# The float64 weights of a recurrence-attention-MLP kernel: converted in the recurrence's last unit but one, and kept in DRAM as float32

## The chip, the cores and the metric

The kernel runs on one core of a Trainium2 chip. The core has five engines, each with a queue of its own that it works through in order: TensorE (PE, matrix products; its weight loads are listed as PEld), VectorE (DVE), ScalarE (ACT), GpSimd (POOL) and SyncE (SP), which here only issues transfers (DMAs). Engines wait for each other through semaphores. The metric is the time of one execution on the device in microseconds (us).

## What is computed

Three parts, one behind the other, in float32:

```python
# r, k, v, w, a, b: (4, 8, 768, 40)
for t in range(S):                                   # recurrence, per batch and head
    y[:, :, t] = rt @ state
    Sa = state @ at
    state = state * wt - outer(Sa, bt) + outer(vt, kt)
x = y as (4, 768, 320)
# mixture of attention experts: x @ w_gate picks 2 of 4 experts; each is causal attention
out += weight_e * (softmax(causal(q_e k_e^T / 8)) @ v_e) @ wo[e]
# gated MLP with mixing over the sequence
h = relu(out @ w_in);  u, v = h[..., :512], h[..., 512:]
v_s = w_spatial @ layernorm(v) + b_spatial
result = (u * v_s) @ w_out
```

`w_in` (320 x 1024) and `w_out` (512 x 320) arrive as float64; all else is float32.

## The kernel before

**The recurrence** (`recurrence`) cuts the sequence into chunks of 64 positions. Two batches with eight heads go together; three chunks make a unit, and there are 8 units (counted from 0), so 24 steps. For each unit a preparation `p1` builds what the steps need, one unit ahead and more: among it `p_l` and `p_sub`, the solve of triangular 32 x 32 systems for all heads at once: 31 pairs of DVE instructions, `sub = L * X` (L227) and `X = X - sub` (L229), each pair on the result of the last. All their operands lie in SBUF. A step `p2` carries the state: PE makes a product, ACT copies it back (`wsb`, L374, L391, L400; `VU`, L393, L407), PE uses it for the next, and at its end DVE adds and scales the new state `SV` (L419, L420), with which the next step's products begin (L370). Beside the state, the outputs of the step before are made: `am` on DVE is a product under a mask (L322), PE needs it in L333 and L341, and `xs` (L344) is stored to `xd` in DRAM.

**Order.** PE's order is written out by hand (`manual_schedule`): after each part of a step `pump` is called, five times a step, 15 times a unit; it runs what of `p1` is due, and other work. The orders of DVE, ACT, POOL and SP are decided when the program is built, by a scheduler that estimates times. On the chip each engine then works through its row in order, and an instruction that waits holds up all behind it.

**Beside the last two units.** In unit 6, whose three steps are the last with a solve in them (that of unit 7), `pump` also advances `pre()`: it loads and splits the weights `wq`, `wk`, `wv`, `w_gate` (`attn_prep`: twelve loads of L629 and L630, then casts and subtractions on DVE, `wv_h`, `wq_l` and so on) and the first batch of x (`first_x`: `xf`, `xh`, `xl`). In unit 7 the attention of batch 0 runs between the steps (`tail`), and `wout_prep` makes `wu_h` and `wu_l` of `w_out`, in four pieces of 128 x 320.

**Behind the recurrence** the rest of that attention is blended with `mlp_prep`, which loads `b_spatial` and `wo`, multiplies `wo` with `w_in` on PE (L701) into `wc_h` and `wc_l` (twelve pieces of `w_in`, 256 columns each), and turns `w_spatial` (L713). Then MLP and attention of the four batches are blended until the end.

**The conversion** of one piece of float64 is `load_f64`: a load of the raw words on SP (L572), three ACT instructions (L578, L579, L581: low word scaled, sign, magnitude), four on DVE (L582 to L585, the bit work) and three on POOL (L586 to L588, products and sum in float32). POOL's take two operands from SBUF and write SBUF.

```python
hi = raw.bitcast(F32).rearrange("p (n w) -> p n w", w=2)[:p, :, 1]
nc.scalar.mul(m, lo, 2.0 ** -52)
nc.vector.tensor_scalar(ei, ti, 1, 0x7F800000, op0=OP.logical_shift_right, op1=OP.bitwise_and)
nc.gpsimd.tensor_mul(m, m, e)
```

## Time and profile before

| | us |
|---|---|
| median of 3 runs | 1215.08 |
| lowest, highest | 1214.11, 1222.42 |
| the profiled execution | 1223.75 |
| its span, first to last instruction | 1222.0 |

Busy time of the span: PE 1024.8 us (84%), DVE 761.9 (62%), ACT 652.1 (53%), POOL 203.0 (17%). Unit 6 lies at about 562 to 627 us, unit 7 at 627 to 735, the attention's tail behind it to about 747, the preparation of the MLP to about 816, then the blended main part.

A row of the timeline gives an instruction's start and duration in us, the engine, the line, what it writes and reads, how many instructions are merged in the row, and in brackets the time the engine had stood before it and what ended that. PEclk is the TensorE clock that was granted, as a share of its full 2.4 GHz; 0.50 is its lower level of 1.2 GHz.

### The profile page before, as it was taken

The page shows a single profiled execution, that of the slowest core. Times are in us where ns is not written, and L with a number is a line of the kernel's source. Part 1 is how long each engine was busy: PE and PEld are TensorE (multiplying, and loading weights), DVE is VectorE, ACT ScalarE, POOL GpSimd, SP SyncE. Part 2 cuts the span into 40 slices and gives each one's busy share as a digit, 9 for nine tenths or more (in the row PEclk, how much of TensorE's full clock was granted, in tenths as well). Part 3 has the DMA queues.
Part 4 walks back from the last instruction along what each step waited for, and adds up shares of the span by engine and source line. Part 5 has one row for each costly group of instructions (what it writes and reads, how often), then busy time and mean ns, then how long its engine had stood idle before and what let it go on. Part 6 is the DMA issues. An engine that isn't in the chain of part 4 may idle for free.

```text
span 1222.0 us, 31926 instructions
## 1 busy us (share of the span) xinstructions
PE 1024.8 (84%) x12730; PEld 896.5 (73%) x12730; DVE 761.9 (62%) x1930; ACT 652.1 (53%) x1599; POOL 203.0 (17%) x381
## 2 busy tenths in 40 slices
PE   5757787787887969879797877798999899999998
PEld 3546676777776868768685665576898798789888
DVE  4586739467495474854835446988657656765650
ACT  2345564655645557465455445667555556555641
POOL 5011000010010100000002015802211211121131
PEclk9999767666766566676675766799999999989999
DMA  4333343333333333323211103210000001000000
GB/s 64 61 63 62 53 67 62 54 57 55 69 60 57 56 52 69 64 45 80 53 41 33 28 7 107 68 39 1 18 32 17 1 17 49 1 1 17 18 1 33
DMA packets 214663, 52.96 MB, mean 43 GB/s; under 512 B 204785, under 2 KB 210673, under 8 KB 214514
## 3 DMA queue, kind: packets, MB, share of 16 engines
q1 hardware_dynamic: 214514, 50.92, 21.2%
q8 instruction: 100, 1.64, 0.6%
q14 instruction: 49, 0.40, 0.1%
HBM read 39.07 MB, written 7.86 MB: 38 GB/s over the span
## 4 chain that ended last, share of the span: by engine, by line
PE 48%; DVE 28%; ACT 14%; issue 5%; DMA 3%; POOL 2%; SPq 1%; ACTq 0%; DVEq 0%; POOLq 0%
DVE X L229 5%; DVE sub L227 5%; PE mm L952 4%; PE mm L953 4%; PE mm L954 4%; ACT XTD L196 3%; ACT XTD L241 3%; PE p L141 2%; PE mp L911 2%; PE y L333 2%; PE mp L841 2%; PE pw L404 2%; PE y L341 2%; ACT f L881 2%; PE p L217 2%
## 5 line engine op out<-in xcount | busy, mean ns | idle before, releaser
L141 PE MATMUL p<-ident,slab 96*128 96x96 f32 x512 | 102.4, 340 | 43.7 <-ACT XTD L197 20.0
L141 PEld LDWEIGHTS p<-ident,slab 96*128 96x128 f32 x512 | 73.7, 194 | 60.7 <-ACT XTD L197 22.4
L227 DVE TENSOR_TENSOR sub<-L,X 96x31 f32<-96x31 f32 (+15 forms) x248 | 83.4, 336 | 17.0 <-ACT L L218 10.5
L196 ACT COPY XTD<-p 32x192 f32<-32x192 f32 x64 | 30.6, 479 | 110.4 <-DVE WL L193 109.9
L229 DVE TENSOR_TENSOR X<-X,sub 96x31 f32<-96x31 f32 (+15 forms) x248 | 83.1, 335 | 6.0
L881 ACT ACTIVATE f<-sc,nm 128x512 f32<-128x512 f32 (+2 forms) x110 | 59.4, 544 | 31.6 <-DVE nm L876 14.4
L602 DVE TENSOR_TENSOR ptl<-mp,pth 128x256 fp32r<-128x256 f32 (+2 forms) x126 | 57.0, 460 | 23.1 <-ACT pth L601 22.1
L876 DVE TENSOR_REDUCE nm<-sc 128x1 f32<-128x512 f32 (+2 forms) x110 | 54.6, 505 | 22.9 <-PE sc L874 18.6
L333 PE MATMUL y<-RT,S 40*40 40x64 f32 (+1 forms) x768 | 49.5, 308 | 22.4 <-DVE am L322 22.4
L159 DVE TENSOR_TENSOR_SCAN PP<-W,scan 104x390 f32<-104x390 f32 x32 | 30.9, 966 | 58.4 <-ACT W L157 58.4
L601 ACT CAST pth<-mp 128x256 fp32r<-128x256 f32 (+2 forms) x126 | 50.0, 409 | 32.3 <-PE mp L911 18.4
L202 POOL COPY PEN<-PP 40x6 f32<-40x6 f32 x64 | 25.7, 401 | 245.0 <-DVE PP L159 243.6
L333 PEld LDWEIGHTS y<-RT,S 40*40 40x40 f32 (+1 forms) x768 | 43.2, 194 | 25.6 <-DVE am L322 23.7
L193 DVE TENSOR_TENSOR WL<-p,mask 64x384 f32<-64x384 f32 x32 | 17.9, 560 | 67.6 <-PE xt L189 67.1
L316 PE MATMUL y<-RT,vut 40*64 40x64 f32 x1536 | 48.1, 259 | 12.2 <-ACT S L383 11.8
L911 PE MATMUL mp<-ident,f 128*128 128x128 f32 x294 | 51.5, 295 | 4.6 <-DVE f L897 2.3
L920 PE MATMUL pa<-pth,vv 128*128 128x256 f32 x168 | 47.5, 297 | 5.9 <-DVE at L932 3.8
L316 PEld LDWEIGHTS y<-RT,vut 40*64 40x64 f32 x1536 | 37.7, 164 | 19.0 <-ACT S L383 14.7
L952 PE MATMUL mm<-ws_h,vn_h 128*128 128x384 f32 x144 | 49.2, 341 | 0.4 <-ACT vn_h L601 0.3
L171 DVE TENSOR_TENSOR kb<-p,RPE 104x384 f32<-104x384 f32 x64 | 35.2, 554 | 22.4 <-PE p L141 20.9
L897 DVE TENSOR_SCALAR f<-f,sm 128x128 f32<-128x128 f32 (+2 forms) x96 | 45.3, 513 | 5.9 <-POOL sm L889 5.3
L953 PE MATMUL mm<-ws_l,vn_h 128*128 128x384 f32 x144 | 48.6, 338 | 0.0
(284 smaller groups left out, 3122.1 us busy)
## 6 DMA issues: line engine op xcount, KB each, us to landing
slab<-in_w_dram SPq DMA_DIRECT2D x128, 30.0 KB
slab<-in_b_dram SPq DMA_DIRECT2D x128, 30.0 KB
slab<-in_k_dram SPq DMA_DIRECT2D x128, 30.0 KB
slab<-in_a_dram SPq DMA_DIRECT2D x128, 30.0 KB
SV<-in_v_dram SPq DMA_DIRECT2D x48, 80.0 KB
VU<-in_v_dram SPq DMA_DIRECT2D x48, 80.0 KB
RR<-in_r_dram SPq DMA_DIRECT2D x48, 80.0 KB
WL<-ABD SPq DMA_DIRECT2D x64, 60.0 KB
```

Of the source, the lines that this page charges most:

```text
L141: nc.tensor.transpose(pt[:, s, :], SLAB[n % NSL][:, s].rearrange("p h d -> p (h d)"), ident[:TS, :TS])
L196: nc.scalar.copy(TD[:, :, g, n].rearrange("j t c -> j c t"), pt[gs, :, gs])
L227: nc.vector.tensor_mul(tv, L[:, j + 1:, j:j + 1].to_broadcast([96, n, m]), X[:, j:j + 1, :m].to_broadcast([96, n, m]))
L229: nc.vector.tensor_sub(X[:, j + 1:, :m], X[:, j + 1:, :m], tv)
L316: nc.tensor.matmul(pas[h][js, q, p], st["vut", q][HR[h], p, js], rt[q][HR[h], p], start=True, stop=True)
L333: nc.tensor.matmul(st["py"][q][hr.start:hr.start + m, p], s0[q][hr, p, :m], rt[q][hr, p], start=(p == 0), stop=False, skip_group_check=True)
L602: (lo_eng or nc.vector).tensor_sub(lo, src, hi.bitcast(F32))
L876: nc.vector.tensor_reduce(nm[:, z:z + 1], sc[:, :nn], op=OP.max, axis=AX.X, negate=True)
L881: nc.scalar.activation(pe[:, n0:n0 + nn], scs[z][:, :nn], AF.Exp, bias=nm[:, :1], accum_out=sm[:, z, i - i0:i - i0 + 1])
L911: nc.tensor.transpose(pp[:, j, z * 128:(z + 1) * 128], pes[z][:, (j0 + j) * 128:(j0 + j + 1) * 128], ident)
L952: nc.tensor.matmul(ps_, ah, bh, start=first, stop=False)
L953: nc.tensor.matmul(ps_, ah, bl_, start=False, stop=False)
```

## The change

All sixteen conversions are made in unit 6, one piece at each of its 15 `pump` calls and what is left at its end, with 320 columns to a piece and 64 in the last of a row of `w_in` (13 pieces of 320 columns, 3 of 64). Each result is stored to DRAM (`wof`, `wif`), and `wout_prep` and `mlp_prep` load float32 from there. The tiles of the conversion are two deep (`bufs=2`) and lie where the recurrence's first pool was.

```diff
@@ -76,7 +76,7 @@
     early = ExitStack()
     ep = early.enter_context(tc.tile_pool(name="rep", bufs=1))
 
-    first = ExitStack()
+    first, convert = ExitStack(), ExitStack()
     ap = first.enter_context(tc.tile_pool(name="rap", bufs=1))
 
     units = [(bb, u) for bb in range(B // BQ) for u in range(NU)]
@@ -490,6 +490,8 @@
             if state["raw"] and not any(x[2] in "wbka" for x in when):
 
                 state["raw"] = False
+                cv = convert.enter_context(tc.tile_pool(name="conv", bufs=2))
+                state["conv"] = pre(cv)
                 state["prep"] = pre()
                 next(state["prep"])
             elif state["prep"] is not None:
@@ -498,15 +500,18 @@
                     with tc.issue_after(marks["v"]):
                         for _ in range(PRN):
                             next(state["prep"], None)
+            if state.get("conv") is not None:
+                next(state["conv"], None)
             if tailq is not None:
                 tailq(TPC / 100)
 
         for c in range(CQ):
             outs.append(y_items(i * CQ + c))
             p2(i * CQ + c, pump)
-        if state["prep"] is not None:
-            for _ in state["prep"]:
+        for x in ("prep", "conv"):
+            for _ in state.get(x) or ():
                 pass
+        convert.close()
     _, _, amat, ys, yk = outs[-1]
     for f in (lambda: amat(0), lambda: amat(1), ys, yk):
         f()
@@ -693,7 +698,7 @@
         win = st.tile([128, 768], F32, name="big").rearrange("p (k f) -> p k f", k=3)
         nc.gpsimd.memset(win[64:, 2], 0.0)
         for k, (k0, kn) in enumerate(KT):
-            load_f64(nc, st, nc.sync, w_in[k0:k0 + kn, f * 256:(f + 1) * 256], win[:kn, k], 256)
+            nc.sync.dma_start(win[:kn, k], w_in[k0:k0 + kn, f * 256:(f + 1) * 256])
             yield 1.0
         for a in range(2):
             pt = bank([128, 256], MMB, "mm")
@@ -724,7 +729,7 @@
     wu_h, wu_l = c["wu_h"], c["wu_l"]
     for a in range(FH // 128):
         x = st.tile([128, DM], F32, name="f64x", bufs=1)
-        load_f64(nc, st, nc.sync, w_out[a * 128:(a + 1) * 128, :], x, DM)
+        nc.sync.dma_start(x, w_out[a * 128:(a + 1) * 128, :])
         yield 1.0
         split(wu_h[:, a], wu_l[:, a], x, nc.gpsimd)
         yield 1.0
@@ -1090,7 +1095,24 @@
         def bank(shape, n=MPB, name="mp"):
             return banks[-1](shape, n, name)
 
-        def pre():
+
+        wif = dp.tile(list(w_in.shape), F32, name="wif")
+        wof = dp.tile(list(w_out.shape), F32, name="wof")
+
+        def converted(st):
+            for src, dst in ((w_out, wof), (w_in, wif)):
+                for p0, pn in chunks(src.shape[0]) if src is w_in else [(p, 128) for p in range(0, FF // 2, 128)]:
+                    for n0 in range(0, src.shape[1], 320):
+                        nn = min(320, src.shape[1] - n0)
+                        x = st.tile([128, 320], F32, name="f64x")[:pn, :nn]
+                        load_f64(nc, st, nc.sync, src[p0:p0 + pn, n0:n0 + nn], x, nn)
+                        nc.sync.dma_start(dst[p0:p0 + pn, n0:n0 + nn], x)
+                        yield
+
+        def pre(cv=None):
+            return converted(cv) if cv is not None else prepared()
+
+        def prepared():
             kp = stages["attn"].enter_context(tc.tile_pool(name="mwa", bufs=1, side="right"))
             with tc.tile_pool(name="staging", bufs=3, side="right") as st:
                 yield from attn_prep(tc, kp, st, c, wq, wk, wv, w_gate, ident)
@@ -1106,7 +1128,7 @@
             parts["attn"], parts["mlp"], parts["prog"] = moe_mlp(
                 tc, xd, c, bank, E, HD, FF, out, ident, k2, k3, parts["kx"], parts["x"][0], ml)
             wp = stages["attn"].enter_context(tc.tile_pool(name="mwu", bufs=1, side="right"))
-            parts["wout"] = wout_prep(tc, wp, stages["wout"].enter_context(tc.tile_pool(name="staging", bufs=WOB)), c, w_out)
+            parts["wout"] = wout_prep(tc, wp, stages["wout"].enter_context(tc.tile_pool(name="staging", bufs=WOB)), c, wof)
             state = {"hops": 0, "credit": 0.0, "spent": 0.0, "safe": True}
 
             def first():
@@ -1155,7 +1177,7 @@
             def rest():
                 cp = stages["mlp"].enter_context(tc.tile_pool(name="mwm", bufs=1))
                 with tc.tile_pool(name="staging2", bufs=STC) as st:
-                    yield from later(mlp_prep(tc, cp, st, bank, c, wo, w_in, w_sp, b_sp, w_out, ident))
+                    yield from later(mlp_prep(tc, cp, st, bank, c, wo, wif, w_sp, b_sp, w_out, ident))
                 ml[1] = stages["second"].enter_context(tc.tile_pool(name="mml", bufs=1))
                 ml[2] = stages["second"].enter_context(tc.tile_pool(name="mml2", bufs=2))
```

Behind the third hunk, as far as `wout_prep`, lines of the change are those of the kernel before plus 5: L582 reads L587 there; L419 stays L419. Where the order changes, on DVE at the end of unit 6's first step (`SV` is the state; `sub` and `X` are the solve; `xs` the outputs; `f64t`, `f64e` the conversion). Before:

```order
L227 TENSOR_TENSOR sub<-L,X 96x247
L344 TENSOR_TENSOR xs<-y,PP_100 104x256
L229 TENSOR_TENSOR X<-X,sub 96x19x13
L227 TENSOR_TENSOR sub<-L,X 96x252
L229 TENSOR_TENSOR X<-X,sub 96x18x14
L419 TENSOR_TENSOR SV_115<-pw,SV_114 40x8x40
L419 TENSOR_TENSOR SV_117<-pw,SV_116 40x8x40
L227 TENSOR_TENSOR sub<-L,X 96x255
L420 TENSOR_TENSOR SV_115<-SV_115,PEN_103 40x8x40
L420 TENSOR_TENSOR SV_117<-SV_117,PEN_103 40x8x40
```

The same place in the change:

```order
L587 TENSOR_SCALAR f64t<-f64t 128x320
L227 TENSOR_TENSOR sub<-L,X 96x247
L588 TENSOR_SCALAR f64t<-f64t 128x320
L419 TENSOR_TENSOR SV_117<-pw,SV_116 40x8x40
L419 TENSOR_TENSOR SV_119<-pw,SV_118 40x8x40
L587 TENSOR_SCALAR f64t<-f64t 128x320
L229 TENSOR_TENSOR X<-X,sub 96x19x13
L589 TENSOR_SCALAR f64e<-f64t 128x320
L420 TENSOR_TENSOR SV_117<-SV_117,PEN_105 40x8x40
L420 TENSOR_TENSOR SV_119<-SV_119,PEN_105 40x8x40
```

Instructions of the third and fourth piece now stand around the state's update, and eight of the first two further up. Of the conversion's 64 DVE instructions 48 stand in unit 6 ahead of the `am` of its third step.

On ACT in the same step, where `VU` and `wsb` are copies of PE's products and `f64raw` are the loaded words. Before:

```order
L391 COPY wsb_8036<-pw 32x320
L391 COPY wsb_8038<-pw 32x320
L393 COPY VU_112<-pw 32x8x40
L393 COPY VU_113<-pw 32x8x40
L400 COPY wsb_8036<-pw 32x320
L400 COPY wsb_8038<-pw 32x320
```

In the change:

```order
L393 COPY VU_114<-pw 32x8x40
L393 COPY VU_115<-pw 32x8x40
L583 ACTIVATE f64m<-f64raw 128x320
L584 ACTIVATE f64s<-f64raw 128x320
L586 ACTIVATE f64t<-f64raw 128x320
L583 ACTIVATE f64m<-f64raw 128x320
L584 ACTIVATE f64s<-f64raw 128x320
L586 ACTIVATE f64t<-f64raw 128x320
L400 COPY wsb_8038<-pw 32x320
L400 COPY wsb_8040<-pw 32x320
```

Six instructions that wait for a load stand between two copies of the step's chain.

On DVE early in the preparation of the MLP (`woT` is `wo` turned, `nm` and `f` are attention, `ptl` and `wc_l` are low parts of split results). Before:

```order
L691 COPY woT<-mm 64x256
L583 TENSOR_SCALAR f64t<-f64t 128x256
L582 TENSOR_SCALAR f64t<-f64t 128x256
L897 TENSOR_SCALAR f<-f,sm 128x384
L897 TENSOR_SCALAR f<-f,sm 128x512
L584 TENSOR_SCALAR f64e<-f64t 128x256
L582 TENSOR_SCALAR f64t<-f64t 64x256
L583 TENSOR_SCALAR f64t<-f64t 128x256
L932 TENSOR_TENSOR at<-pa,ah 64x256
```

In the change:

```order
L696 COPY woT<-mm 64x256
L902 TENSOR_SCALAR f<-f,sm 128x384
L902 TENSOR_SCALAR f<-f,sm 128x512
L881 TENSOR_REDUCE nm<-sc 128x1
L884 TENSOR_TENSOR nm<-nm 128x1
L937 TENSOR_TENSOR at<-pa,ah 64x256
L607 TENSOR_TENSOR wc_l<-mm,wc_h 128x256 x2
```

The 48 instructions of the conversion are gone from here, and the first `wc_l` stands right behind the turned `wo`.

## Rows read from the trace of the kernel before

**Rows 1.** page, chain that ended last, share of the span by engine

```profile
PE 48%; DVE 28%; ACT 14%; issue 5%; DMA 3%; POOL 2%; SPq 1%; ACTq 0%; DVEq 0%; POOLq 0%
```

**Rows 2.** start:end, length, busy us (instructions) of PE, PEld, DVE, ACT, POOL, PEclk, DMA

```profile
568.00:582.00 14.00, 12.14 (x228) 10.78 (x222) 12.91 (x37) 5.08 (x12) 0.00 (x0) 0.57 0.38 83
582.00:594.00 12.00, 7.79 (x174) 6.61 (x174) 11.67 (x31) 3.97 (x10) 1.10 (x2) 0.57 0.28 60
594.00:612.00 18.00, 15.02 (x310) 12.96 (x309) 13.68 (x36) 9.82 (x21) 0.73 (x1) 0.69 0.26 50
627.00:747.00 120.00, 97.20 (x1134) 77.06 (x1131) 53.40 (x139) 56.02 (x146) 19.38 (x38) 0.67 0.11 25
747.00:803.00 56.00, 42.84 (x194) 33.24 (x193) 50.62 (x121) 38.35 (x106) 36.32 (x55) 0.75 0.36 106
803.00:816.00 13.00, 12.64 (x99) 11.83 (x98) 10.38 (x31) 8.74 (x23) 0.99 (x3) 1.00 0.11 32
```

**Rows 3.** timeline of DVE in unit 6

```profile
568.20 0.20 DVE L227 TENSOR_TENSOR sub<-L,X 96x31 f32<-96x31 f32 x1 [6.34 <-ACT L L218]
580.01 1.00 DVE L419 TENSOR_TENSOR SV<-pw,SV 40x320 f32<-40x320 f32 x2
593.08 1.29 DVE L322 TENSOR_TENSOR am<-y,mask 128x512 f32<-128x512 f32 x2
602.58 1.01 DVE L419 TENSOR_TENSOR SV<-pw,SV 40x320 f32<-40x320 f32 x2 [0.42 <-PE pw L416]
609.02 0.55 DVE L599 CAST xh<-xf 64x768 fp32r<-64x768 f32 x1 [2.94 <-DMA xf<-xd]
610.59 1.29 DVE L322 TENSOR_TENSOR am<-y,mask 128x512 f32<-128x512 f32 x2
```

**Rows 4.** chain that ended last, unit 6: start, us, what

```profile
593.82 1.92 PE y L333 x30
```

**Rows 5.** groups of DVE, 568 to 622 us: count, busy, mean ns, idle before

```profile
L227 DVE TENSOR_TENSOR sub<-L,X 96x31 f32<-96x31 f32 (+15 forms) x31 | 10.5, 337 | 7.2 <-ACT L L218 6.3
L229 DVE TENSOR_TENSOR X<-X,sub 96x31 f32<-96x31 f32 (+15 forms) x31 | 10.4, 335 | 0.7
L602 DVE TENSOR_TENSOR xl<-xf,xh 128x768 fp32r<-128x768 f32 x2 | 1.9, 950 | 0.0
```

**Rows 6.** groups in unit 7, forms apart: prices of a conversion's instructions

```profile
L585 DVE TENSOR_SCALAR f64t<-f64t 128x320 int32<-128x320 int32 x4 | 1.3, 324 | 0.1
L588 POOL TENSOR_TENSOR f64x<-f64t,f64s 128x320 f32<-128x320 f32 x4 | 3.5, 864 | 0.3
L578 ACT ACTIVATE f64m<-f64raw 128x320 f32<-128x320 uint32 x4 | 2.0, 490 | 0.0
```

**Rows 7.** the same view, instructions on tile f64t alone: DVE, ACT, POOL

```profile
627.00:747.00 120.00, 5.13 (x16) 1.92 (x4) 6.90 (x8) 0.67 0.11 25
747.00:803.00 56.00, 22.51 (x48) 5.14 (x12) 20.33 (x24) 0.75 0.36 106
```

**Rows 8.** timeline of DVE, then of POOL, in the preparation

```profile
772.49 0.29 DVE L584 TENSOR_SCALAR f64e<-f64t 128x256 int32<-128x256 int32 x1
772.70 2.36 DVE L602 TENSOR_TENSOR xl<-f,xh 128x768 fp32r<-128x768 f32 x2
772.92 1.31 POOL L586 TENSOR_TENSOR f64m<-f64m,f64e 128x256 f32<-128x256 f32 x1 [1.68 <-DVE f64e L584]
774.21 1.43 POOL L588 TENSOR_TENSOR big<-f64t,f64s 64x256 f32<-64x256 f32 x1
776.74 0.73 POOL L588 TENSOR_TENSOR big<-f64t,f64s 128x256 f32<-128x256 f32 x1
```

**Rows 9.** timeline of SP and of ACT in unit 6; chain at 747 us

```profile
569.01 0.61 SPq L630 DMA_DIRECT2D wvg<-in_moe_w_gate_dram  x1
571.80 0.86 ACT L400 COPY wsb<-pw 32x320 f32<-32x320 f32 x2 [1.38 <-PE pw L397]
747.66 4.76 DMA f64raw<-in_moe_w_in_dram
```

## The prediction

> **What bounds the kernel now.** I read the page first, then the busy time by stretch, then the queues of the engines one by one. By the page the chain that ended last is 48% TensorE (PE) and 28% VectorE (DVE) [rows 1]. Such shares mix stages, so the question is which engine ends the waits in the two stretches that the change touches: the one that receives the conversion (unit 6, counted from 0; about 562 to 627 us) and the one that loses most of it (747 to 803 us, the preparation of the second half, between the end of the recurrence and the first dense part).
>
> In unit 6 the table of stretches shows DVE busy for 12.91 of 14 us, 11.67 of 12 and 13.68 of 18, with PE granted about 0.57 to 0.69 of its clock and GpSimd (POOL) nearly idle [rows 2]. The timeline of DVE says the same row by row [rows 3]: from the first instruction of the triangular solve at 568.20 to the mask product `am` of the third step at 610.59 the one pause that counts is 2.94 us at 609.02, for a load. Inside this stretch stand the state updates of L419 at 580.01 and 602.58, on which the next step's first matmuls depend: a step is 22.57 us. PE's products of L333 at 593.82 follow directly on the `am` that stood in DVE's queue behind the solve [rows 4]. So here DVE is a bound: whatever is put into its queue ahead of a state update or an `am` lengthens the step. The solve itself is 62 instructions of 0.34 us, 20.9 us [rows 5].
>
> From 747 to 803 us DVE is busy for 50.62 of 56 us, PE for 42.84 at a granted clock of 0.75, ACT for 38.35, POOL for 36.32; after 803 us PE takes over with 12.64 of 13 us at 1.00 [rows 2]. The conversion's four DVE instructions are 48 there, 22.51 us [rows 7].
>
> **What the change removes from 747 to 803.** Without the 22.51 us DVE has 28.1 us of work left and is no bound. PE is next. It cannot do its part in less than 42.84 us if its clock stays as it was; were it at 1.00 throughout, about 0.75 x 42.84 = 32 us. A stage that was 56 us becomes one of between 42.84 / 0.9 = 48 us (some PE idle left, as before) and 33 us. The gain lies between 8 and 23 us. I take 15: the loads now bring half the bytes and convert nothing, so the 4.76 us of waiting for a float64 load at 747.66 [rows 9] goes too, but attention's own back-and-forth between engines stays. The stage after it is PE at full clock and gains nothing.
>
> **What it removes from the last unit (627 to 747).** Sixteen DVE instructions, 5.13 us [rows 7], where DVE is busy for 53.40 of 120 us [rows 2]. Most of that was beside other work: between 0 and 5.1, I take 2. At the end of the recurrence ACT now meets `bs`, which waits for a load, between two copies that attention needs: 0 to 2 us lost, I take 1.
>
> **What it adds to unit 6.** Sixteen pieces: 13 of 320 columns, 3 of 64. Each is a load, 3 ACT, 4 DVE and 3 POOL instructions and a store.
>
> First, a wait. The order of ACT puts six conversions between L393 and L400, and DVE's has two of L582 (L587 in the change) early in the solve. The loads that they wait for are issued behind the twelve loads of L629 and L630, the last of which goes out at 569.01 for 0.61 us [rows 9]. With 0.5 us to issue the second and the 4.76 us that such a load took at 747.66, its data is there at about 575.0; three ACT instructions of 0.49 us [rows 6] end at about 576.5. L400, at 571.80 before [rows 9], cannot start until then, and behind it are queued the copies that PE's products of L404 wait for; DVE, which would be at about 572.9, stands too. Cost: 4 us (3 to 5).
>
> Second, DVE's own instructions. By the order 12 of the 16 pieces stand ahead of the third step's `am`: 40 instructions of 320 columns and 8 of 64. At 0.324 us [rows 6] and nearly no gap 40 cost 13.2; the 8 are between nothing and the same, I take 1.6. Together 14.8.
>
> Third, POOL. In this kernel POOL's two-operand instructions and part of DVE's do not run at the same time. Two instructions of L602 (both inputs in SBUF) begin at 772.70 and end at 775.06, 1.22 us each, where the same form took 0.95 with POOL idle [rows 5, 8]; POOL's next to them took 1.31 and 1.43, against 0.73 for one with nothing beside it [rows 8]. Each waits for the other to end. The conversion's DVE instructions took 22.51 / 48 = 0.47 us there; one with a free way took 0.29 [rows 8], so some 9 us were lost to 36 POOL instructions, 0.25 for each, in a stage where about half of DVE's work reads PSUM and goes on. In unit 6 nearly all of it reads SBUF alone, the solve (two SBUF inputs) included. I take 0.5 for each of the 34 POOL instructions that fall before the third `am` (36 of twelve pieces, the last two behind it): 17 us. Lower bound: only the conversion's own instructions are held up, 48 x 0.19 = 9. Upper bound: DVE stands for each of them in full, 28 x 0.864 [rows 6] and 6 short ones of, say, 0.3: 26.
>
> The Trainium skill, in SBUF — State Buffer, section "Who interferes with whom", states this as a rule: a DVE instruction with two SBUF inputs contends with a GpSimd instruction that reads SBUF, as does a copy, cast or `tensor_scalar` in a two-port mode, and the second to issue blocks until the first ends. By that rule the 62 instructions of the solve are held up, which the rows of L602 suggest and no row of the solve itself shows; the sum with it is the one below, without it about 8 us less.
>
> Against this, the pause of 2.94 us before the third `am` is filled [rows 3]: -2.9. Behind that `am` are four more pieces; one of their L582 waits for ACT, which has it behind eight copies of L241, and the state update of L419 is queued behind it on DVE. Then the outputs of the unit's last step, finished at once, wait for an `am` that is late too. A few microseconds of slack take some of it: 0 to 5, I take 4.
>
> SP gets 32 more transfers. Its stores wait for POOL, and loads of `VU`, `SV` and `RR` are queued behind them; these are wanted one step of some 22 us later, and I cost them at nothing. Should a store be late by a step, that cover is gone and the delay counts in full.
>
> Sum for unit 6: 4 + 14.8 + 17 - 2.9 + 4 = 37 us; by the lower ends 3 + 13.2 + 9 - 2.9 + 0 = 22, by the upper 5 + 14.8 + 26 + 0 + 5 = 51.
>
> **Sum.** 37 - 15 - 2 + 1 = +21 us. The profiled execution took 1223.75 us (span 1222.0), so it would be 1245; the median of the three runs is 1215.08, and on that the forecast is 1236.
>
> **Rivals.**
> *Forecast, 55%: DVE and POOL in each other's way, the preparation gives back less than half.* 1236, from 1225 to 1247.
> *Not slower, 27%: the solve is not held up by POOL.* Then unit 6 costs 4 + 14.8 + 9 - 2.9 + 2 = 27, and if PE in the preparation then runs dense and its clock rises, giving 23 instead of 15, the sum is 27 - 23 - 2 + 1 = +3: 1218. For it: no row shows a solve instruction next to a busy POOL, and PE was at 1.00 from 803 us on [rows 2]. Against it: L602 with two SBUF inputs was held up [rows 8]. It decides when unit 6 costs under 28 us at a gain of 16.
> *Much slower, 13%: the pace of the pieces.* The buffers are two deep, so the third piece's first instructions wait for POOL's last on the first, and DVE and ACT, which run in order, wait with them, as do the loads behind SP's stores. Then POOL's whole work counts, unit 6 costs 46 to 51, the preparation gives 10: 1215 + 50 - 10 - 1 = 1254. Against it: 36 us of POOL work has some 90 us.
> *Faster, 5%: the conversion does lie in gaps.* Unit 6 must cost under 12 us, for instance the 4 us wait and 8 us of instructions in the third step, where DVE is less busy after 612 us; with a gain of 23 and 2: 1215 + 12 - 25 = 1202. Against it: by the order four fifths of the DVE instructions stand before the third `am`, where DVE has no gap.
>
> **How the numbers follow.** A measurement of this kernel can tell about 1%, 12 us, from no change. The first and third case lie nearly all above 1227: slower 0.68. The second, with the lowest part of the first: within 1% 0.27. Faster 0.05. The likeliest case alone reaches from 1225 to 1247; to hold 8 in 10 the range takes in most of the second and part of the third: 1213 to 1254.
>
> **What would show each step.** In the profile after: the first sub of the solve at about 568 as now; L400 of that step at about 576 with ACT idle before the first conversion, for a DMA; the state updates of L419 more than 28 us apart instead of 22.57; solve instructions whose mean is well above 0.34 us (0.5 or more if POOL holds them up); DVE without idle time until the end of unit 6; the recurrence's end 30 us or more later. In the preparation: DVE no longer the busiest, PE over 85% busy, the stage 8 to 23 us shorter. I am wrong if the solve's mean stays at 0.34, if DVE shows idle time in unit 6, or if the preparation becomes shorter by more than 25 us.

## The result, and the profile after

| | us |
|---|---|
| before, median of 6 runs (lowest, highest) | 1217.03 (1214.11, 1222.42) |
| the change, median of 6 runs (lowest, highest) | 1231.27 (1228.26, 1236.05) |
| ratio, 95% interval | 1.0112 (1.009 to 1.0134) |
| the profiled execution of the change, its span | 1236.05, 1234.3 |

The change is slower by 1.1%, some 14 us; forecast were 21. Below, a ratio r is turned into microseconds as (r - 1) x 1217.

The two spans differ by 12.3 us. They can be split at marks that both traces have: the first `sub` of the solve in unit 6, the third state update after it, and the last `xs` (L344).

| stretch | before | after | difference |
|---|---|---|---|
| start to first `sub` of unit 6 | 568.20 | 566.07 | -2.1 |
| from there to the third state update (unit 6) | 51.78 | 82.40 | +30.6 |
| from there to the last `xs` (unit 7) | 116.33 | 114.33 | -2.0 |
| from there to the end | 485.69 | 471.50 | -14.2 |

The timeline of DVE shows these marks in the change (before: [rows 3]). Brackets hold the time DVE had stood, and for what:

```profile
566.07 0.20 DVE L227 TENSOR_TENSOR sub<-L,X 96x31 f32<-96x31 f32 x1 [5.91 <-ACT L L218]
572.70 0.33 DVE L587 TENSOR_SCALAR f64t<-f64t 128x320 f32<-128x320 f32 x1 [1.96 <-ACT f64t L586]
...
585.54 1.00 DVE L419 TENSOR_TENSOR SV<-pw,SV 40x320 f32<-40x320 f32 x2
...
605.70 0.70 DVE L587 TENSOR_SCALAR f64t<-f64t 128x320 f32<-128x320 f32 x1 [3.84 <-ACT f64t L586]
606.44 1.29 DVE L322 TENSOR_TENSOR am<-y,mask 128x512 f32<-128x512 f32 x2
...
619.25 1.00 DVE L419 TENSOR_TENSOR SV<-pw,SV 40x320 f32<-40x320 f32 x2
...
635.15 1.29 DVE L322 TENSOR_TENSOR am<-y,mask 128x512 f32<-128x512 f32 x2
...
648.23 0.32 DVE L587 TENSOR_SCALAR f64t<-f64t 64x320 f32<-64x320 f32 x1 [4.14 <-ACT f64t L586]
648.47 1.00 DVE L419 TENSOR_TENSOR SV<-pw,SV 40x320 f32<-40x320 f32 x2
```

The second and the third step took 22.57 and 17.40 us before; now they take 33.71 and 29.22. And DVE, which had hardly a pause in the stretch where it was called the bound, now has several, for ACT. The table of stretches, columns as in [rows 2], shows the three steps before:

```profile
568.20:580.01 11.81, 11.08 (x216) 9.92 (x211) 10.95 (x33) 3.92 (x9) 0.00 (x0) 0.50 0.42 92
580.01:602.58 22.57, 16.21 (x311) 13.76 (x310) 21.06 (x59) 10.55 (x23) 1.10 (x2) 0.62 0.24 49
602.58:619.98 17.40, 15.44 (x313) 13.86 (x314) 7.11 (x15) 9.45 (x21) 0.73 (x1) 0.64 0.26 49
```

The same in the change:

```profile
566.07:585.54 19.47, 11.93 (x218) 10.26 (x214) 14.79 (x39) 10.11 (x23) 6.56 (x6) 0.58 0.51 136
585.54:619.25 33.71, 18.97 (x312) 16.33 (x312) 29.54 (x74) 15.41 (x36) 21.93 (x19) 0.50 0.39 107
619.25:648.47 29.22, 17.41 (x312) 15.48 (x312) 19.97 (x50) 17.81 (x45) 18.94 (x20) 0.56 0.37 92
```

DVE is busy for 14.79 of 19.47, 29.54 of 33.71 and 19.97 of 29.22 us. In the third step it had been busy for only 7.11 of 17.40 us before, so that it bounded two steps of the three. PE's granted clock, lower in the second and third step, explains little: the chain's products of L387, L397 and L404 took 1.26 to 1.28 us in all three steps, before and after; those of L416 went from 0.81 to 1.30 us in the second step and from 1.28 to 0.98 in the third. DVE's groups over the unit (count, busy, mean ns, idle before) answer to [rows 5]:

```profile
L229 DVE TENSOR_TENSOR X<-X,sub 96x31 f32<-96x31 f32 (+15 forms) x31 | 14.9, 480 | 0.4
L227 DVE TENSOR_TENSOR sub<-L,X 96x31 f32<-96x31 f32 (+15 forms) x31 | 13.6, 437 | 6.2 <-ACT L L218 5.9
L587 DVE TENSOR_SCALAR f64t<-f64t 128x320 f32<-128x320 f32 (+3 forms) x16 | 5.3, 333 | 14.1 <-ACT f64t L586 13.3 <-POOL f64m L591 0.8
```

The solve costs 28.5 us instead of 20.9, and 14.1 us pass in front of the conversion's first DVE instruction. ACT, for which DVE waits there, waits itself. The waits of ACT in the unit (what waited, for what: us in total, times, longest):

```profile
ACT f64m L583 <- POOL f64t L592: 17.9, 9, 5.8
ACT wsb L374 <- PE pw L370: 5.5, 1, 5.5
ACT f64m L583 <- DMA f64raw<-in_moe_w_out_dram: 4.4, 2, 3.2
ACT f64s L584 <- POOL f64x L593: 4.3, 5, 2.4
```

ACT stands 26.6 us (17.9 + 4.4 + 4.3) in front of conversion instructions: a tile of the piece before the last is still with POOL, or the load is not there. The copies `wsb` and `VU`, from which PE makes the next state, stand in the same row behind them. Such a place in the second step, on ACT:

```profile
590.88 0.86 ACT L374 COPY wsb<-pw 32x320 f32<-32x320 f32 x2 [5.53 <-PE pw L370]
...
602.61 0.49 ACT L583 ACTIVATE f64m<-f64raw 128x320 f32<-128x320 uint32 x1 [5.84 <-POOL f64t L592]
603.13 0.84 ACT L391 COPY wsb<-pw 32x320 f32<-32x320 f32 x2
```

The same two copies in the kernel before:

```profile
583.41 0.86 ACT L374 COPY wsb<-pw 32x320 f32<-32x320 f32 x2 [1.99 <-PE pw L370]
...
587.10 0.84 ACT L391 COPY wsb<-pw 32x320 f32<-32x320 f32 x2 [2.16 <-PE pw L387]
```

From L374 to L391 it is 12.25 us instead of 3.69. And why POOL was late, first POOL's row, then DVE's last instruction in that time:

```profile
598.05 4.52 POOL L592 TENSOR_TENSOR f64t<-f64t,f64m 128x320 f32<-128x320 f32 x1 [2.20 <-DVE f64t L590]
```

```profile
601.45 0.40 DVE L227 TENSOR_TENSOR sub<-L,X 96x255 f32<-96x255 f32 x1
```

POOL's instruction, 0.86 us when alone, took 4.52. DVE began ten instructions without a pause in that time, each some 0.08 us before the one ahead had ended; the last ended at 601.85, and POOL's 0.72 us later. Then the ring closes: DVE stands for ACT (3.84 us at 605.70, shown above), ACT for POOL, and POOL had stood for DVE.

With the copies on ACT as marks (before and after, us from mark to mark) the 30.6 us divide so:

| step | stretch | before | after | more | what ACT stood for in it |
|---|---|---|---|---|---|
| 1 | first `sub` to L400 | 3.60 | 9.09 | 5.5 | two loads, 4.4 |
| 1 | L400 to L419 | 8.21 | 10.38 | 2.2 | POOL, 2.5 at three places |
| 2 | L419 to L374 | 3.40 | 5.34 | 1.9 | PE |
| 2 | L374 to L391 | 3.69 | 12.25 | 8.6 | POOL, 0.5 + 2.4 + 5.8 |
| 2 | L391 to L419 | 15.48 | 16.12 | 0.6 | POOL, 0.6 |
| 3 | L419 to L374 | 3.20 | 7.80 | 4.6 | POOL, 1.3 + 4.9 |
| 3 | L374 to L391 | 3.41 | 4.44 | 1.0 | POOL, 1.2 |
| 3 | L391 to L400 | 3.07 | 6.38 | 3.3 | POOL, 2.1 |
| 3 | L400 to L419 | 7.72 | 10.60 | 2.9 | POOL, 1.0 |

The last column says what ACT stood for, and not in each row is that the cause. In two rows the state update itself was late in DVE's row. PE's last products for it, in the first step and in the third:

```profile
580.05 1.28 PE L416 MATMUL pw<-VU,KBT 128*40 128x40 f32 x32
...
643.40 0.98 PE L416 MATMUL pw<-VU,KBT 128*40 128x40 f32 x32
```

In the first step they were ready at 581.33, and L419 began at 585.54, 4.2 us later (0.8 before): it stood behind instructions of the solve that took 0.72 to 0.95 us beside POOL. In the third they were ready at 644.38, and L419 began at 648.47: it stood behind the L587 at 648.23, which waited 4.14 us for ACT, and ACT had that piece behind eight copies of L241 (4.16 us from 643.09).

### The profile page after: what moved, and what is told of

Same layout as the page of the kernel before. It is cut to its first block, busy times and chain, and to the rows that moved or that the text cites. A ratio compares the mean times of both kernels' runs of the same rounds, so it can differ in the third digit from the quotient of the medians.

```text
span 1234.3 us, 32027 instructions
## 1 busy us (share of the span) xinstructions
PE 1021.0 (83%) x12730; PEld 896.6 (73%) x12730; DVE 763.5 (62%) x1930; ACT 654.4 (53%) x1599; POOL 210.9 (17%) x381
## 3 DMA queue, kind: packets, MB, share of 16 engines
q1 hardware_dynamic: 218610, 54.85, 21.3%
## 4 chain that ended last, share of the span: by engine, by line
PE 46%; DVE 27%; ACT 15%; issue 6%; DMA 3%; SPq 1%; POOL 1%; ACTq 0%; POOLq 0%; DVEq 0%
DVE sub L227 5%; DVE X L229 5%; PE mm L957 4%; PE mm L958 4%; PE mm L959 4%; ACT XTD L196 3%; ACT XTD L241 3%; PE p L141 3%; PE mp L916 2%; PE mp L846 2%; ACT f L886 2%; PE y L333 1%; PE p L206 1%; PE pw L404 1%; PE y L341 1%
## 5 line engine op out<-in xcount | busy, mean ns | idle before, releaser
L227 DVE TENSOR_TENSOR sub<-L,X 96x31 f32<-96x31 f32 (+15 forms) x248 | 86.3, 348 | 14.7 <-ACT L L218 8.8
L229 DVE TENSOR_TENSOR X<-X,sub 96x31 f32<-96x31 f32 (+15 forms) x248 | 87.5, 353 | 5.7
L607 DVE TENSOR_TENSOR ptl<-mp,pth 128x256 fp32r<-128x256 f32 (+2 forms) x126 | 57.2, 461 | 21.2 <-ACT pth L606 20.3
L333 PE MATMUL y<-RT,S 40*64 40x64 f32 (+1 forms) x768 | 51.2, 310 | 18.1 <-DVE am L322 18.0
L333 PEld LDWEIGHTS y<-RT,S 40*64 40x64 f32 (+1 forms) x768 | 44.2, 195 | 22.0 <-DVE am L322 20.0
L193 DVE TENSOR_TENSOR WL<-p,mask 64x384 f32<-64x384 f32 x32 | 17.9, 560 | 68.0 <-PE xt L189 67.5
L959 PE MATMUL mm<-ws_h,vn_l 128*128 128x384 f32 x144 | 48.4, 336 | 0.0
```

The lines of the kernel that those rows point to most:

```text
L227: nc.vector.tensor_mul(tv, L[:, j + 1:, j:j + 1].to_broadcast([96, n, m]), X[:, j:j + 1, :m].to_broadcast([96, n, m]))
L229: nc.vector.tensor_sub(X[:, j + 1:, :m], X[:, j + 1:, :m], tv)
L333: nc.tensor.matmul(st["py"][q][hr.start:hr.start + m, p], s0[q][hr, p, :m], rt[q][hr, p], start=(p == 0), stop=False, skip_group_check=True)
L607: (lo_eng or nc.vector).tensor_sub(lo, src, hi.bitcast(F32))
L959: nc.tensor.matmul(ps_, al, bh, start=False, stop=last)
```

## The experiments

The kernel before ran beside each of them; the ratios are to it. The first four ask what the change gives and takes, and what POOL has to do with it.

**No conversion at all.** From the change: `state["conv"]` is never set or advanced, `wout_prep` reads float32 rows of `w_sp`, and

```diff
-            nc.sync.dma_start(win[:kn, k], w_in[k0:k0 + kn, f * 256:(f + 1) * 256])
+            nc.sync.dma_start(win[:kn, k], w_sp[k0:k0 + kn, (f % 3) * 256:(f % 3 + 1) * 256])
```

> Leaves out every conversion: unit 6 is as before the change, and the preparation and w_out's four pieces load float32 of the same size (rows of w_spatial) instead. This is the change's gain without its price. Theory (gain and price add up): from the end of the recurrence to the end the change took 471.5 us, the kernel before 485.7, so about -14, and 2 more in unit 7: 1217 - 16 = 1201 (1197 to 1206). Rival (the preparation's own 27 us, 79.7 against 53.2 to the 816th us, are the gain, and the change gives 12 of them back only because it comes late): 1190.

Measured: ratio 0.9866 (0.983 to 0.9903), -16 us, as the theory had it. Unit 6 took 51.88 us, as before the change, and unit 7 109.1 instead of 116.3.

**The price alone.** The change with `load_f64` put back into `wout_prep` and `mlp_prep`, which read `w_out` and `w_in`; `wof` and `wif` are still written.

> Converts in unit 6 and stores the results, but nobody reads them: unit 7 and the preparation convert for themselves as before. This is the price without the gain. Theory: the third state update of unit 6 comes 30.6 us later after the start of the solve, and all of it reaches the end: 1217 + 30 = 1247 (1242 to 1251). Rival (part of the delay is slack that a later stage takes up, such as a load that is waited for anyway): 1235 or less.

Measured: 1.0275 (1.0249 to 1.0301), +33 us. No stage further on takes any of the delay up. Price and gain add up to +17; the change itself is +14, and the difference lies within the two intervals.

**Without POOL's three instructions.**

```diff
-    nc.gpsimd.tensor_mul(m, m, e)
-    nc.gpsimd.tensor_add(t, t, m)
-    nc.gpsimd.tensor_mul(dst, t, sg)
+    return t
```

> The changed kernel with POOL's three instructions of each conversion left out; what DVE has made of the word is stored. ACT's three and DVE's four stay. Theory (POOL is the larger half of unit 6's price, in two ways: DVE instructions beside it are 0.9 us instead of 0.35, and its own stretch to 3 to 5 us beside the solve, for which ACT and then DVE wait): unit 6 falls from +31 to about +17, the solve's mean is back at 0.34 us, and DVE's waits of 3.8 and 4.1 us at L587 go: 1231 - 14 = 1217 (1212 to 1221). Rival (the price is DVE's own 64 instructions, the wait for the raw words, and SP's and ACT's queues): 1228 to 1231.

Measured: 1.0053 (1.0039 to 1.0066), +6.5 us, so that POOL's instructions are worth 7 of the 30. This lies between the two forecasts. The solve is back at 0.334 us on average, as expected, and the wait for POOL is gone. But in ACT's row others have come:

```profile
ACT f64m L584 <- DMA f64raw<-in_moe_w_in_dram: 15.6, 8, 3.4
ACT f64m L584 <- DMA f64raw<-in_moe_w_out_dram: 5.1, 3, 3.3
ACT f64t L587 <- DMA wif<-f64t: 3.7, 3, 1.7
```

ACT stands 24.9 us here (with 0.5 for DVE), against 26.6. What ends the wait has changed: the load, or the store that frees a buffer.

**POOL's three on DVE.**

```diff
-    nc.gpsimd.tensor_mul(m, m, e)
-    nc.gpsimd.tensor_add(t, t, m)
-    nc.gpsimd.tensor_mul(dst, t, sg)
+    nc.vector.tensor_mul(m, m, e)
+    nc.vector.tensor_add(t, t, m)
+    nc.vector.tensor_mul(dst, t, sg)
```

> The changed kernel with POOL's three instructions of each conversion moved to DVE: POOL is idle in unit 6, DVE has 48 instructions more, some 0.49 us each (between the 0.42 of 128x260 and the 0.69 of 128x512 with two SBUF inputs): up to 23.5 us more in a stage that DVE bounds, 18 of them before the third product under the mask. Theory (without POOL some 14 us of unit 6 go): 1231 - 14 + 18 = 1235 (1230 to 1240). Rival (POOL costs DVE nothing): 1231 + 18 to 23 = 1251.

Measured: 1.0052 (1.003 to 1.0074), +6.3 us, below both forecasts. DVE got 48 instructions more, some 20 us (three groups of 6.6 to 6.7 us), and by the ratio it costs the same as having left them out; unit 6 is 3.1 us longer in the trace (76.30 and 73.19). Priced by their length in a row that is the bound, they would have cost far more. ACT's waits, now for DVE and for loads:

```profile
ACT f64s L584 <- DVE f64x L593: 9.2, 6, 3.6
...
ACT f64m L583 <- DVE f64t L592: 6.0, 5, 2.6
ACT f64m L583 <- DMA f64raw<-in_moe_w_out_dram: 3.8, 2, 3.2
ACT f64m L583 <- DMA f64raw<-in_moe_w_in_dram: 2.3, 1, 2.3
```

The next ones ask what the rest is.

**Load and ACT only.** As without POOL's, and DVE's four left out too (`return t` stands ahead of `tensor_scalar_max`).

> The changed kernel with the conversion cut down further: besides POOL's three, DVE's four instructions are left out too; the load, ACT's three and the store stay. The two runs before show 1202.5 without any conversion and 1225.7 with all but POOL's instructions, so 23 us are left to explain. Theory (they are mostly DVE's own 64 instructions in a stage that DVE bounds, 18.5 us by busy time, of which some 12 on the path; the wait for the first words is 4): 1213 (1209 to 1217). Rival (they are waits: ACT and DVE stand in order for each piece's load or buffer, and the recurrence's copies stand behind them): 1219 to 1225.

Measured: 0.9989 (0.9967 to 1.0011), -1 us, which is 15 us above no conversion. As a time that is 1216, inside the theory's band; but of the 23 us to be explained leaving out DVE's four instructions took away 8, and 15 are left with load, ACT and store. So the larger part is not DVE's, which is the rival's mechanism at less than its price. ACT stands 19.9 us for loads: 14.7 us eight times for pieces of `w_in`, 5.2 us three times for `w_out`.

**Raw words two pieces ahead.** Three buffers for `f64raw`, and the first three loads ahead of the twelve weight loads (of the edit, the loop):

```diff
+            for i in range(len(todo)):
+                while len(raws) < min(i + 2 + 1, len(todo)):
+                    s, _, pn, nn = todo[len(raws)]
+                    raws.append(raw_f64(st, nc.sync, s, pn, nn, 3))
```

> The changed kernel with the raw words loaded two pieces ahead into three buffers, the first three loads ahead of the twelve weight loads. Nothing else is changed. Theory (the first wait for raw words, 4.1 us of DVE's idle time at L587, is on the path, and most later waits are for POOL, which stay): 1231 - 4 = 1227 (1224 to 1229). Rival 1 (the waits for words are the larger part of the price, since nopool shows ACT waiting six more times for a load): 1220 or less. Rival 2 (the wait moves on to the next piece's buffers): 1231.

Measured: 1.0112 (1.0086 to 1.0137), the same as the change; the second rival. The wait for words has shrunk and that for POOL has grown:

```profile
ACT f64m L590 <- POOL f64t L599: 20.3, 8, 7.7
...
ACT f64s L591 <- POOL f64x L600: 6.8, 7, 2.9
...
ACT f64m L590 <- DMA f64raw<-in_moe_w_out_dram: 1.9, 1, 1.9
```

That is 29.0 us in front of conversion instructions.

**POOL alone.** The kernel before, and in unit 6 this instead of the conversion:

```diff
+            for _ in range(16):
+                for _ in range(3):
+                    nc.gpsimd.tensor_mul(d, a, b)
+                yield
```

> The kernel before, where POOL in unit 6 multiplies two constant tiles of 128x320 forty-eight times (48 x 0.86 = 41 us of POOL), and nothing reads the product; no other part of the conversion is there. This is the price of a busy POOL by itself. Theory (DVE and POOL exclude each other on operands in SBUF, and the solve loses what the change's solve lost, 7.6 us, with some idle time taking up a part): slower by 3 to 10 us, rows of L227 and L229 of about 0.9 us in places. Rival (POOL alone waits and gives way): no change, solve rows at 0.34 us on average, POOL rows of several us.

Measured: 1.0171 (1.0152 to 1.019), +21 us, twice the upper end of what I expected. DVE, then POOL:

```profile
567.73 0.90 DVE L229 TENSOR_TENSOR X<-X,sub 96x87 f32<-96x87 f32 x1
568.67 0.93 DVE L227 TENSOR_TENSOR sub<-L,X 96x112 f32<-96x112 f32 x1
...
573.42 1.29 DVE L322 TENSOR_TENSOR am<-y,mask 128x512 f32<-128x512 f32 x2
```

```profile
558.24 21.54 POOL L1108 TENSOR_TENSOR poold<-poola,poolb 128x320 f32<-128x320 f32 x23
```

Twenty-three POOL instructions took 21.54 us, 0.94 each, and from 565.83 on every instruction of the solve beside them 0.90 to 0.93, whatever its width (96x87 took 0.24 alone), but for the one right behind `am` (0.64). One of POOL's and one of DVE's go by turns, and it is DVE that pays: six of the 23 ran before the solve began, and POOL's pace was the same there. POOL's busy time and count in a stretch with DVE idle, and in one beside the solve:

```profile
558.20:563.80 5.60, 5.16 (x6) 0.89 0.82 171
566.70:579.80 13.10, 12.03 (x14) 0.50 0.18 45
```

`am`, one of whose inputs is in PSUM, took its 1.29 as ever. This bears out the Trainium skill, SBUF — State Buffer, section "Who interferes with whom", for the solve itself: a DVE instruction with two SBUF inputs contends with a GpSimd instruction that reads SBUF. A pair took 0.94 us, less than the two by themselves (0.86 and 0.24), so a part of each lies outside the lock.

Unit 6 took 74.11 us here instead of 51.78, the solve 38.3 instead of 20.9, and ACT had no conversion to stand for. The order of DVE is that of the kernel before: 28 and 59 of the solve's 62 instructions stand ahead of the first two state updates in both. So where the order stays, what makes DVE's row longer does make the steps longer.

**ACT alone, loads alone, DVE alone**, each put on the kernel without conversion: ACT's three instructions of each piece on one tile; the load and a store of each piece; DVE's four on two constant tiles, set behind the DVE instruction that was written last ahead of them.

> The kernel of the run without conversion (1202.5, ratio 0.987), plus ACT's three instructions of each piece in unit 6, all on one tile of raw words that is loaded once: no waiting for a load, no store, nothing on DVE and POOL. Loads together with ACT cost 15 us (ratio 0.999). Theory (the cost is the waiting in ACT's queue: a conversion stands there for its load, and the copies of the recurrence stand behind it): ACT's 18 us of work lie in its idle time, ratio 0.987 to 0.991 (1203 to 1208). Rival (the work itself, since ACT's copies are on the chain of the step): ratio 0.996 or more (1214).

Measured: 0.9915 (0.988 to 0.9951), 6 us above no conversion. It was just outside the theory's band, and the one load that it keeps made ACT stand 4.8 us.

> The kernel without conversion again, plus each piece's load of raw words and its store in unit 6, nothing on ACT, DVE and POOL (the stored words are the raw ones, and nothing reads them). Theory (the loads alone keep nobody waiting): ratio 0.987 to 0.989 (1202 to 1206). Rival (SP's queue or the transfers themselves delay the recurrence's own loads): 0.993 or more (1210).

Measured: 1.001 (0.9987 to 1.0033), 17.5 us above no conversion; the rival, and as much as load and ACT together. The first two steps are as before (11.81 and 22.55 us). All is lost at one place in the third:

```profile
622.78 0.55 DVE L604 CAST xh<-xf 64x768 fp32r<-64x768 f32 x1 [19.54 <-DMA xf<-xd]
624.35 1.29 DVE L322 TENSOR_TENSOR am<-y,mask 128x512 f32<-128x512 f32 x2
```

The load of `xf` was issued at 619.40, behind five loads and five stores of pieces that SP was on from 602.04 to 617.36. DVE stood for it 19.54 us, with the step's `am` behind it, and ACT's L407 waited 21.12 us for PE. So this run prices a mishap of SP's row, not the transfers as such; in the change `xf` came in time, and in load and ACT DVE waited 4.4 us for it (2.9 before).

> The kernel without conversion (ratio 0.987), plus DVE's four instructions of each piece in unit 6, on two constant tiles: no loads, nothing on ACT and POOL. This prices the second term of the prediction by itself (14.8 us of instructions less 2.9 of filled idle time, 12). Theory (DVE bounds unit 6, so its instructions count, but a row that does not depend on the one ahead starts every 0.24 us, not every 0.32): 48 x 0.24 less 2.9, about 9: ratio 0.992 to 0.997 (1208 to 1214). Rival (DVE's instructions fall in waits that are there anyway, as 48 more of them cost nothing in the run with POOL's three on DVE): ratio 0.990 or less (1205).

Measured: 0.988 (0.9864 to 0.9897), 2 us above no conversion, and the two intervals overlap; the rival. The instructions stand in DVE's row much as in the change, two rows of state updates of which are

```profile
579.11 1.00 DVE L419 TENSOR_TENSOR SV<-pw,SV 40x320 f32<-40x320 f32 x2
...
602.58 0.48 DVE L419 TENSOR_TENSOR SV<-pw,SV 40x320 f32<-40x320 f32 x1 [0.20 <-PE pw L416]
```

which is 13.26 and 36.73 us behind the first `sub` (565.85), against 11.81 and 34.38 before. DVE is busy for 49.43 of the first 55.15 us of this unit, and the state hardly notices; the third update came 5.4 us later. What is put off is the solve: 24 and 47 of its 62 instructions stand ahead of the first two state updates, where it was 28 and 59. Its last result is wanted by PE's L237 in the third step, and there was room: in the kernel before it was ready at 606.07 and used at 616.15. The third `am`, behind all 62, came 6.8 us later.

The runs side by side (loads alone is left out for its mishap), unit 6 from the first `sub` to the third update, and what ACT stood in front of conversion instructions. Each price carries the interval of the run without conversion, some 4 us either way, besides its own:

| run | price by ratio, us over no conversion | unit 6 | ACT stood |
|---|---|---|---|
| no conversion | 0 | 51.88 | 0 |
| DVE alone | 2 | 57.22 | 0 |
| POOL alone (over the kernel before) | 21 | 74.11 | 0 |
| ACT alone | 6 | 60.19 | 4.8 |
| load and ACT | 15 | 68.41 | 19.9 |
| without POOL's | 23 | 73.19 | 24.9 |
| POOL's on DVE | 23 | 76.30 | 21.3 |
| words ahead | 30 | 79.15 | 29.0 |
| the change | 30 | 82.40 | 26.6 |

**Two versions that should have beaten both kernels**, and did not. The first spreads the sixteen pieces over units 0 to 5, where DVE and ACT stand for PE (the tiles are one deep here, the raw words two; ACT waited for none of them):

```diff
+            if (0 < i < len(units) - 2 or i == 0 and gap > 7) and gap in (1, 11, 14):
+                with behind(tc, "VAP"):
+                    next(conv, None)
```

> A version: the same sixteen pieces are converted one at a time in units 0 to 5, three a unit, at calls 1, 11 and 14 of the fifteen, where the kernel before shows DVE standing 8 to 9 us for PE, with the raw words loaded one piece ahead. Theory (a conversion costs little where DVE and ACT stand anyway, and gain lies at 1202.5): 1206 (1203 to 1212), faster than both kernels. Rival (any conversion in the recurrence costs 1.5 to 2 us a piece, through ACT's and DVE's queues): 1227 to 1234.

Measured: 1.0165 (1.0143 to 1.0188), +20 us; the rival. From 130 to 560 us DVE stood for the conversion thirteen times:

```profile
DVE f64t L595 <- ACT f64t L594: 31.9, 13, 3.5
```

The gaps of 8 to 9 us in a row are the waits of a chain from PE to ACT to DVE and back. An instruction set into such a gap has to be ready when its turn comes, and these were not.

The second leaves `w_in` in the preparation and moves `w_out`'s four pieces out of unit 7, behind `w_spatial`'s turn:

```diff
+                    yield from later(wout_prep(tc, parts["wp"], st, c, w_out), WOE)
```

> A version of the kernel before: w_out's four pieces are converted not in unit 7 but behind w_spatial's turn, where PE is the bound (12.64 of 13 us at 1.00) and ACT and DVE have slack; w_in stays in the preparation. w_out is first needed at 880 us. Without conversion unit 7 was 7.2 us shorter (109.1 against 116.3). Theory (a piece costs about 2 us wherever ACT's and DVE's queues carry a chain, and little where PE is dense): 1217 - 7 + 2 = 1212 (1208 to 1216). Rival (it costs there what it cost in unit 7): 1217 to 1221.

Measured: 1.0098 (1.0062 to 1.0134), +12 us; worse than both forecasts. Unit 7 did become shorter, from its first state update to its last `xs` 89.8 us instead of 94.8. But the MLP is queued behind `w_out` and began later (its first product with `ws_h` at 863.2 instead of 844.2), and in between PE has little but attention:

```profile
800.00:830.00 30.00, 21.96 (x109) 16.28 (x108) 23.26 (x67) 20.72 (x58) 13.34 (x23) 0.86 0.00 1
```

PE is busy for 21.96 of 30 us at a granted clock of 0.86; in the kernel before it was 25.90 of 27 at 1.00 from 803 to 830 us.

## Why the prediction was right, and where its steps were wrong

The sign, the size of the sum and the range held: +21 forecast, +14 measured, 1231 in 1213 to 1254, with 1236 as the likeliest. The terms fared unequally, and that the sum came out so near is in part luck.

**Held.** The first wait: L400 at 576 was forecast, with ACT standing for a load; it came at 575.16 after 4.4 us of standing (5.5 on the path; 4 forecast, 3 to 5). The tail of the unit: 3.9 us from the third `am` to the third update (4 forecast), and in the way forecast, an L587 that waits for ACT behind the copies of L241, with the update behind it. SP at nothing: `xf` was in time, and ACT stood for loads only at the first two pieces (4.4 us); loads alone shows with its 19.54 us what a late one costs. Unit 7: -2.0 (-2), by two amounts that the sum did not have: without any conversion it was 7.2 us shorter, and with the price alone 3.2 longer; the last pieces reach into it. Attention's tail: ACT stood 2.79 us for `bs`, and the next `ptl` waited 3.41 us instead of 1.77 (1 forecast, 1.6 measured). The preparation and all behind it: -14.2 (-15). Unit 6 as a whole: +30.6 (37, from 22 to 51).

**Failed: "whatever is put into its queue ahead of a state update or an `am` lengthens the step", the 14.8 us of DVE's own instructions.** By themselves they cost 2 us (5.4 in the trace of unit 6), and 48 more in the run with POOL's three on DVE cost nothing by the ratio (3.1 in the trace); taken out of the run without POOL's, where they also had ACT to wait for, they gave 8. I priced them by their length, as if all else in a full row kept its place. Most of that row was the solve, whose last result is wanted in the third step only, and the order lets it wait: state updates and the second `am` keep near their place and the solve slides behind them (in the change, too, 25 and 48 of its instructions stand ahead of the first two updates instead of 28 and 59). That the row is a bound where the order stays, POOL alone shows. A sign for it was in [rows 2] already: in the last part of the unit DVE was busy for 13.68 of 18 us.

**Mis-sized: POOL, 17 us.** The exclusion is as the prediction had it, and a POOL stream alone costs 21 us, 0.43 for each of the 48 instructions where 0.5 was taken. In the change the solve lost 7.6 us by it (28.5 instead of 20.9), and POOL's instructions are worth 7 by the runs. The solve is not all of it: with the casts, the low parts and the conversion's own instructions DVE's were longer by some 14 us (an estimate: each that was over 0.1 us longer, against the same shape in runs with POOL idle), of which some lay on the path, as the late update of the first step, and some did not. The other half of the collision I left out: POOL is held up too, and longer. That cost comes through the buffers, which takes the next point.

**Missing from the sum, but named as the third case at 13%: the pace of the pieces.** "The third piece's first instructions wait for POOL's last on the first, and DVE and ACT, which run in order, wait with them": this is what the table of ACT's copies shows, 8.6 + 4.6 + 3.3 us at the three largest places behind the first wait. The case priced it by POOL's whole work, 46 to 51, and was too dear by that; its mechanism has the largest part in the change's trace. The argument against it, 36 us of POOL's work in some 90, counted POOL's work and not the time that a piece takes on its way around the ring. So the sum came out near by errors of opposite sign, which is the luck in it: by the runs that price them alone or leave them out, DVE's instructions counted for some 10 us too much (some 4 by the 8 above) and POOL's exclusion for some 10 too much, and ACT's standing counted for nothing behind the first load.

The experiments do not let the price be shared out among loads, DVE and POOL. Take away what ends the wait in ACT's row and the next one ends it: POOL (26.6 us of standing with it), loads and stores (24.9 without POOL's instructions), DVE's products (21.3), POOL again (29.0 with the words ahead). What is common is the row: three conversion instructions on ACT that are not ready, with the step's copies behind them. That this standing is the price is read from the traces and from the table, where the two go together; no run keeps the conversion and takes the standing away, and POOL alone costs 21 us without any. A ring of more than two buffers for all the tiles was not tried.

**The signs that were to be looked for.** Solve instructions at 0.5 or more were forecast if POOL holds them up: 0.44 and 0.48 over the unit, since only some stand beside POOL. DVE "without idle time until the end of unit 6" was wrong, 14.1 us, and I had named that as a sign that I would be wrong: it was, of the mechanism. State updates more than 28 us apart: 33.71 and 29.22. End of the recurrence 30 us later: 26.5, from 736.31 to 762.80 at the last `xs`. In the preparation:

```profile
775.00:803.00 28.00, 26.66 (x159) 22.80 (x158) 22.19 (x56) 18.77 (x52) 2.14 (x10) 0.96 0.37 118
803.00:816.00 13.00, 10.82 (x75) 8.19 (x76) 12.12 (x30) 11.24 (x31) 0.60 (x3) 1.00 0.11 31
```

PE is the busiest, 26.66 of 28 us, at a granted clock of 0.96. But the stage became shorter by more than the 8 to 23 us that were named: from the last `xs` to the last product of `wo` with `w_in` 35.1 us instead of 60.8, and these 25.7 are also past the 25 that was named as a sign of being wrong. This is not all gain. From the last `xs` to the 816th us PE has done 259 instructions instead of 317, since attention got fewer turns beside a shorter preparation; the 58 that are left were done later, and at the end -14.2 remain. A stage in which two streams are blended is to be measured by what is left to do at its end; the 8 to 23 came right as the sum, not as the stage.

## What to carry over

What is added to a full row costs its length only if all else in the row keeps its place: ask for each busy instruction when its result is used and whether the order can put it off, and try the added instructions alone, without their waits, before pricing them by their length. What lengthens the instructions that are there, in an order that stays, counted nearly in full (POOL alone). On engines that work in order, what also costs is an instruction that is not ready, ahead of one that a chain waits for; with two buffers in a ring over three engines there was one in each run that had the ring, and when its cause was removed the next took its place. Work set into a gap must be ready when the gap opens.

## What the runs showed of the hardware

DVE and POOL lock each other out by turns or for long, depending on DVE's row. In the solve each instruction needs the result of the last and there are some 0.03 us between them: POOL gets in at each. In POOL alone it kept 0.94 us from start to start beside the solve, its pace with DVE idle too, and DVE's instructions took 0.90 to 0.93 us instead of 0.2 to 0.4. At three places in the change instructions that are independent of each other, as the conversion's are, stand in between; each began before the one ahead had ended, and POOL waited until the first pause and ended 0.72 to 0.73 us behind it: 4.52, 3.37 and 4.81 us for an instruction of 0.86. A pause is not always needed: POOL's L591 at 593.68 (1.18 us) ended 0.72 us behind an L607 whose successor had begun 0.08 us before its end. What decides between the two was not tested. At the three places independent work between the links of a chain kept DVE busy and starved POOL. The change shows both within 25 us; the beginning of a stretch of the first kind, DVE and then POOL:

```profile
577.59 0.35 DVE L229 TENSOR_TENSOR X<-X,sub 96x192 f32<-96x192 f32 x1
577.98 0.92 DVE L227 TENSOR_TENSOR sub<-L,X 96x207 f32<-96x207 f32 x1
578.93 0.92 DVE L229 TENSOR_TENSOR X<-X,sub 96x207 f32<-96x207 f32 x1
```

```profile
576.93 2.69 POOL L591 TENSOR_TENSOR f64m<-f64m,f64e 128x320 f32<-128x320 f32 x2 [22.47 <-DVE f64e L589]
```
